# Loads by head and a prologue by head pair in a fused block-sparse attention and gated FFN kernel

## The chip, the cores and the metric

The kernel runs on one core of a Trainium2 chip. The metric is the device time of one execution in microseconds; of several executions the median is taken. TensorE is called PE in the profile (PEld is its weight load), VectorE DVE, ScalarE ACT, GpSimd POOL and SyncE SP.

## What is computed

Attention over 4 batches, 8 heads, 768 positions and head size 64, and behind it a gated feed-forward layer over the 3072 tokens. Each query sees the keys less than 16 positions away, and 24 block summaries of the whole sequence (the maximum of k and the mean of v over blocks of 32 positions):

```python
    k_sum = k.reshape(B, H, nb, block, D).max(axis=3)
    v_sum = v.reshape(B, H, nb, block, D).mean(axis=3)
    scores_l = scale * np.matmul(q, k.transpose(0, 1, 3, 2))
    mask_l = np.abs(pos[:, None] - pos[None, :]) < window
    scores_s = scale * np.einsum('bhsd,bhnd->bhsn', q, k_sum) + np.log(block)
...
    attn = np.matmul(a, np.concatenate([v, v_sum], axis=2))
    # x: attn as [3072, 512]
    ffn_out = gelu(x @ w_gate) * (x @ w_val) @ w_out
    out = x + sigmoid(x @ w_res) * ffn_out
```

Inputs and output are float32 in DRAM; the kernel loads everything as bfloat16[...] and accumulates in float32.

## The kernel before

The work is cut into eight units, half a batch each (384 tokens, six query tiles of 64). For a query tile the keys are its own 64, 16 on each side (the rims) and the 24 summaries, laid side by side in `kW` (128 columns per tile and head pair) and in `vext` (one row per key, for each tile and head 64 values, a column of ones at index 64, and padding up to 96). `kW`, `qT` and `vext` exist twice, for even and odd batches. Heads are handled in pairs: `s_step` computes the transposed scores of one pair for six tiles and their exponentials `P` on ACT, `av_step` (in the first unit `av_first`, in two parts: the band rows, and the summary rows from `vblk`) multiplies by v, `av_end` divides by the sum, and `xt_step` turns the result for the feed-forward part.

The feed-forward part of a unit is twelve steps `fo`. Each step makes a tile g (x times 128 columns of w_gate) and a tile vv (the same of w_val) with four matmuls of 384 columns each; ACT takes the Gelu of g into `ge`, and DVE multiplies by vv into `gvT` (the product of this step). g, vv and several others share four PSUM tiles (`ps_mm`), and `ge` has three buffers. Then come the w_res and w_out matmuls, mixed with the attention of the next unit (`first_out`, `mid_out`). The order on each engine is the order of the program text (`tc.manual_schedule`); each engine works its own queue in order and waits by semaphores.

Unit 0 is special. It has a prologue of its own that turns k and q by PE transposes, makes the block maxima (`k_blocks`) and rims (`k_rims`, `own_rims`) on DVE and the block means by matmul (`vsum_mm`), with `keep_warm` matmuls on a zero tile in between. The band mask `mneg` (0 inside the band, -240000 outside) is built by POOL with four `affine_select`, and is added to the scores of pairs 0 and 1 by a matmul; for pairs 2 and 3 DVE multiplies `P` by `maskt`, which is derived from `mneg`. During the twelve steps of unit 0, `unit0_extras(fo)` puts constants and copies for later onto DVE, behind the product of step `fo`. In the first steps of unit 1, `k_place` puts the turned k of batch 1 in its place. Batches 2 and 3 get k by DMA transposes from `k_nat`.

All loads are issued by POOL in the order of the text: k of batch 0 in two halves by heads, q for the first half sequence, v in twelve blocks of 64 positions (all heads each), the first piece of w_gate among the v blocks; then the pieces of w_val and w_gate in turns, the second q, w_res, w_out, and the data of batch 1.

Of the kernel before, what the change touches and what calls it, by code (L numbers as in the profile page):

```python
# [8 lines left out]
F32 = mybir.dt.float32  # L9
BF16 = mybir.dt.bfloat16  # L10
# [5 lines left out]
def kernel(  # L16
# [50 lines left out]
    mneg = const.tile([128, 128], BF16, name="mneg")  # L67
    vblk = const.tile([128, H, D + 1], BF16, name="vblk")
# [22 lines left out]
    def k_tile():  # L91
        return qk.tile([PP, H, PJ, D], BF16, tag="k_sb", name="k_sb")

    def load_q(half, j):
        t = qk.tile([TU // j, H, j, D], BF16, tag="q_sb", name="q_sb")
        nc.gpsimd.dma_start(
            out=t.rearrange("p h j d -> p h (j d)"),
            in_=q[0, :, half * TU:(half + 1) * TU].rearrange("h (p j) d -> p h (j d)", j=j))
        return t

    def v_loads(b, lo=0, hi=NT):
        for t in range(lo, hi):
            nc.gpsimd.dma_start(out=vext[b % 2][0:QT, t, :, 0:D],  # L103
                                in_=v[b, :, t * QT:(t + 1) * QT, :].rearrange("h p d -> p h d"))
# [9 lines left out]
    def load_k_nat(b):  # L114
        k_nat = qk.tile([QT, NT, DM], BF16, tag="k_nat", name="k_nat")
        for t in range(NT):
            nc.gpsimd.dma_start(out=k_nat[:, t].rearrange("p (h d) -> p h d", d=D),  # L117
                                in_=k[b, :, t * QT:(t + 1) * QT, :].rearrange("h p d -> p h d"))
        return k_nat
# [15 lines left out]
    with tc.manual_schedule():  # L135
# [23 lines left out]
        def load_w(w, src, c):  # L159
# [9 lines left out]
        k_sb[0] = k_tile()  # L169
        load_k(0, k_sb[0], 0, 2)  # L170
        nc.gpsimd.affine_select(out=ident[:], in_=ident[:], compare_op=ALU.not_equal, fill=1.0,
                                base=0, pattern=[[-1, 128]], channel_multiplier=1)
        load_k(0, k_sb[0], 1, 2)
        q_sb[0] = load_q(0, QJ)
        nc.scalar.activation(vext[0][0:QT, :, :, D + 1:VP],
                             warm[0:QT, 0:1].unsqueeze(1).unsqueeze(1).to_broadcast([QT, NT, H, VP - D - 1]),
                             AF.Copy)
        vext_consts(0)
        v_loads(0, 0, 6)
        for cols, sign, base in ((slice(0, QT), 1, WIN - 1), (slice(0, QT), -1, WIN - 1),  # L180
                                 (slice(QT, QT + WIN), 1, WIN - 1 - QT), (slice(QT + WIN, BAND), -1, -1)):
            m = mneg[0:QT, cols]
            nc.gpsimd.affine_select(out=m, in_=m, compare_op=ALU.is_ge, fill=-240000.0, base=base,
                                    pattern=[[-sign, cols.stop - cols.start]], channel_multiplier=sign)
        v_loads(0, 6, 7)
        load_w(w_gate, wg_src, 0)
        v_loads(0, 7, NT)
        kw_consts(0)
        own_keys(bmat, NT)
        nc.vector.memset(vblk[96:128, :, D:D + 1], 1.0)  # L190
        nc.vector.memset(vext[1][0:QT, :, :, D + 1:VP], 0.0)


        for c in range(6):
            if c:
                load_w(w_gate, wg_src, c)
            load_w(w_val, wv_src, c)
            if c == 4:
                q_sb[1] = load_q(1, QJ)
# [53 lines left out]
        def own_rims(lo, hi, after):  # L253
            x = vext[0]
            if after:
                hi = min(hi, NT - 1)
                nc.vector.tensor_copy(x[QT:QT + WIN, lo:hi, :, 0:D], x[0:WIN, lo + 1:hi + 1, :, 0:D])
            else:
                lo = max(lo, 1)
                nc.vector.tensor_copy(x[QT:BAND, lo:hi, :, 0:D], x[QT - 2 * WIN:QT, lo - 1:hi - 1, :, 0:D])  # L260

        def vsum_mm(b, vs, lo, hi):
            for t in range(lo, hi):
                for i in range(2):
                    nc.tensor.matmul(vs[i][96:128, 0:DM // 2], bmat[:, t, :],
                                     vext[b % 2][0:QT, t, 4 * i:4 * i + 4, 0:D],
                                     start=(t == 0), stop=(t == NT - 1))
# [19 lines left out]
        def s_mm(u, hp, s):  # L287
            b, half = u // 2, u % 2
            kw, qt = kW[b % 2], qT[b % 2]
            if u == 0 and hp < 2:  # L290
                for hh in range(2):
                    nc.tensor.matmul(s[hh], mneg[:],
                                     ident[:, 0:QT].unsqueeze(1).to_broadcast([128, HT, QT]),
                                     start=True, stop=False, skip_group_check=True)
            for t in range(HT):
                tt = half * HT + t
                for hh in range(2):
                    ps = slice(hh * 64, hh * 64 + 64)
                    nc.tensor.matmul(s[hh][:, t * QT:(t + 1) * QT], kw[ps, tt, hp, :],  # L299
                                     qt[ps, tt // 2, hp, (tt % 2) * QT:(tt % 2 + 1) * QT],  # L300
                                     start=(u > 0 or hp > 1), stop=True,
                                     skip_group_check=True)

        def s_step(u, hp, st, banks=None):
            if banks:
                s = [p.tile([128, 512], F32, tag=tag, name="s") for p, tag in banks]
            else:
                s2 = ps_s.tile([128, 2, 512], F32, tag="s", name="s")
                s = [s2[:, hh] for hh in range(2)]
            s_mm(u, hp, [x[:, 0:TU] for x in s])  # L310
            P = ppool.tile([128, 2, HT, QT], BF16, tag="P", name="P")
            if banks:
                for hh in range(2):
                    nc.scalar.activation(P[:, hh].rearrange("p t q -> p (t q)"), s[hh][:, 0:TU], AF.Exp,  # L314
                                         scale=scale, bias=bias_t[:])
            else:
                nc.scalar.activation(P.rearrange("p a t q -> p a (t q)"), s2[:, :, 0:TU], AF.Exp,  # L317
                                     scale=scale, bias=bias_t[:])
            if u or hp > 1:
                Pf = P.rearrange("p a t q -> p (a t) q")  # L320
                nc.vector.tensor_mul(Pf, Pf, maskt.unsqueeze(1).to_broadcast([128, 2 * HT, QT]))  # L321
            st["P", hp] = P
# [133 lines left out]

        keep_warm(12)
        k_step(0, 0, ps_mm, "mm")
        k_step(0, 1, ps_mm, "mm")
        keep_warm(6)  # L460
        k_step(0, 2, ps_mm, "mm")
# [3 lines left out]
        k_step(0, 3, ps_mm, "mm")  # L465
        keep_warm(5)
        tq = [turn_pair(q_sb[0], hp, turn_tile(q_sb[0], ps_mm, "mm")) for hp in range(NP)]
        for hp in range(3):
            q_place(0, hp, tq[hp])
        st = new_unit()  # L470
        vs = [ps_t.tile([128, 512], F32, tag="t", name="vs"), ps_o.tile([128, 512], F32, tag="ao", name="vs")]
        s_step(0, 0, st)
        q_place(0, 3, tq[3])
        s_step(0, 1, st, MM2)
        own_rims(0, HT, False)
        own_rims(0, HT, True)
        vsum_mm(0, vs, 0, 3)
        s_step(0, 2, st)
        s_step(0, 3, st, MM2)
        vsum_mm(0, vs, 3, 8)  # L480
        keep_warm(1)
        gvT = upool.tile([128, FO, TU], BF16, tag="gvT", name="gvT")
        ao = [ps_mm.tile([128, NSUB, 2, D + 1], F32, tag="mm", name="ao") for _ in range(NP)]
        for hp in range(3):
            av_first(hp, st, ao[hp], 0, BAND)
        vsum_mm(0, vs, 8, NT)
        nc.vector.tensor_copy(vblk[96:128, 0:H // 2, 0:D],
                              vs[0][96:128, 0:DM // 2].rearrange("p (h d) -> p h d", d=D))
        nc.scalar.copy(vblk[96:128, H // 2:H, 0:D],
                       vs[1][96:128, 0:DM // 2].rearrange("p (h d) -> p h d", d=D))  # L490
        nc.scalar.activation(gate1[:], bias_t[0:1, :], AF.Gelu)
        av_first(3, st, ao[3], 0, BAND)
        keep_warm(1)
        for hp in range(4):
            av_first(hp, st, ao[hp], BAND, 128)
            av_end(hp, st, ao[hp])
        keep_warm(1)
        turn = [dict(pool=ps_t, tag="t", copy=nc.scalar.copy), dict(pool=ps_o, tag="ao", copy=nc.scalar.copy)]
        xt_step(0, 0, st, **turn[0])
        keep_warm(1)  # L500
        xt_step(0, 1, st, **turn[1])
        g0, v0 = mm_tile("g"), mm_tile("vv")
        gv_mm(g0, w_gate, st, 0, (0,))
        gv_mm(v0, w_val, st, 0, (0,))
        xt_step(0, 2, st, **turn[0])
        gv_mm(g0, w_gate, st, 0, (1,))
        gv_mm(v0, w_val, st, 0, (1,))
        g1, v1 = mm_tile("g"), mm_tile("vv")
        gv_mm(g1, w_gate, st, 1, (0, 1))
        xt_step(0, 3, st, **turn[1])  # L510
# [12 lines left out]
        def unit0_extras(fo):  # L523
            if fo == 2:
# [85 lines left out]
        for u in range(NU):  # L610
# [9 lines left out]
            for fo in range(0 if u else 2, FO):  # L620
# [22 lines left out]
                if half == 1 and nb < B:  # L643
# [11 lines left out]
                    if nb == 1:  # L655
                        if fo == 0:
                            tk = turn_all(k_sb[nb])
                        if fo < NP:
                            k_place(nb, fo, tk[fo])
                    elif 2 <= fo < 2 + NP:  # L660
                        k_blocks(nb, fo - 2)
# [36 lines left out]
```

The softmax here doesn't subtract the row's maximum and nothing guards it: scores larger than these inputs give would overflow.

## Time and profile before

| what | value |
|---|---|
| median of 10 runs | 257.25 us (256.88 to 257.84) |
| profiled execution, its own time | 257.4 us |
| its span | 255.6 us |
| PE busy | 248.2 us, 97% of the span |
| DVE busy | 158.0 us, 62% |
| ACT busy | 126.9 us, 50% |
| POOL busy | 111.1 us, 43% |
| v loads (L103) | 48 issues, 741 ns each on POOL |
| k_nat loads (L117) | 24 issues, 732 ns each |
| granted TensorE clock | 9 tenths or more in every slice |

The profile shows one execution. A row of the timeline gives the start and the length in us, the engine, the line of the kernel, the operation, what it writes and reads with their shapes, and in brackets the idle time of the engine before it and what ended it. The chain of waits is the sequence of work that ended last, followed back from the end; a row of it gives the start, the length and who was at work. Busy time of an engine that nobody waits for costs nothing.

### The profile page before, as it was taken

To read this page: it belongs to the slowest core of one execution; us is meant where nothing else is said; L and a number is where in the kernel's file an instruction comes from. 1 tells how busy PE (TensorE), PEld (TensorE's weight loads), DVE (VectorE), ACT (ScalarE), POOL (GpSimd) and SP (SyncE) were. 2 spreads that over 40 slices of the span, in tenths; PEclk is the share of its full clock that TensorE was granted. 3 is DMA by queue.
4 is the path that set the end of the run, shared out by engine and by line. 5 is a ranking of instruction groups with operands and counts; after the bars stand their busy time and mean duration, and the time that the engine had idled before them with its cause. 6 is when DMAs were issued, how large, how long until landed. Compare 5 with 4: busy or idle time off the path is not lost.

```text
span 255.6 us, 5803 instructions
## 1 busy us (share of the span) xinstructions
PE 248.2 (97%) x2277; PEld 138.4 (54%) x2300; DVE 158.0 (62%) x350; ACT 126.9 (50%) x212; POOL 111.1 (43%) x155
## 2 busy tenths in 40 slices
PE   8999999999999999999999999999999999999994
PEld 2665654565554555546654665545554565455543
DVE  5975776399477544767567544867567544854424
ACT  6676359266493338344482338244482337253320
POOL 8897552293345986265405995157404000000000
PEclk9999999999999999999999999999999999999999
DMA  5999999999913999989603999959903500240003
GB/s 79 179 141 169 197 201 208 191 163 184 144 22 98 170 109 146 121 136 178 120 13 95 177 112 153 103 132 165 139 15 78 136 0 3 50 138 0 0 3 123
DMA packets 98475, 29.34 MB, mean 115 GB/s; under 512 B 83592, under 2 KB 95312, under 8 KB 98352
## 3 DMA queue, kind: packets, MB, share of 16 engines
q0 software_dynamic: 68720, 14.76, 69.2%
q1 hardware_dynamic: 29728, 14.21, 24.9%
q8 instruction: 18, 0.29, 0.5%
q14 instruction: 9, 0.07, 0.1%
HBM read 29.36 MB, written 6.29 MB: 139 GB/s over the span
## 4 chain that ended last, share of the span: by engine, by line
PE 80%; DMA 10%; DVE 4%; POOL 3%; issue 2%; POOLq 0%; DVEq 0%
PE f L423 23%; PE vv L375 21%; PE g L375 21%; PE r L413 8%; DMA w_val<-in_moe_w_val_dram 4%; DMA w_gate<-in_moe_w_gate_dram 3%; PE ao L335 3%; DMA q_sb<-in_q_dram 3%; PE s L299 3%; POOL vext L103 2%; DVE th L429 1%; DVE o L432 1%; PE vs L273 1%; POOL w_val L161 1%; POOL w_gate L161 1%
## 5 line engine op out<-in xcount | busy, mean ns | idle before, releaser
L381 DVE TENSOR_TENSOR gvT<-ge,vv 128x384 bf16<-128x384 f32 x96 | 52.6, 552 | 50.7 <-PE vv L375 46.3
L380 ACT ACTIVATE ge<-g 128x384 f32<-128x384 f32 x96 | 46.9, 490 | 69.4 <-DVE gvT L381 36.4
L375 PE MATMUL vv<-xT,w_val 128*128 128x384 bf16 x384 | 78.7, 326 | 0.4 <-DMA w_val<-in_moe_w_val_dram 0.3
L375 PE MATMUL g<-xT,w_gate 128*128 128x384 bf16 x384 | 78.8, 326 | 0.1
L423 PE MATMUL f<-w_out,gvT 128*128 128x512 bf16 x262 | 62.7, 380 | 1.5 <-issue 1.1
L375 PEld LDWEIGHTS <-w_gate 128*128 128x128 bf16 x384 | 37.1, 98 | 26.7 <-issue 1.8
L375 PEld LDWEIGHTS <-w_val 128*128 128x128 bf16 x384 | 37.4, 98 | 25.4 <-DMA w_val<-in_moe_w_val_dram 0.7
L423 PEld LDWEIGHTS <-gvT 128*128 128x128 bf16 x276 | 25.6, 98 | 29.6 <-DMA w_out<-in_moe_w_out_dram 0.3
L103 POOL DMA_DIRECT2D vext<-in_v_dram x48 | 33.5, 741 | 13.4 <-DMA w_out<-in_moe_w_out_dram 5.6
L416 ACT ACTIVATE th<-r 128x512 f32<-128x512 f32 x24 | 13.5, 605 | 27.5 <-PE r L413 27.5
L429 DVE SCALAR_TENSOR_TENSOR th<-th,f 128x512 f32<-128x512 f32 (+2 forms) x26 | 16.6, 640 | 14.1 <-PE f L423 14.1
L321 DVE TENSOR_TENSOR P<-P,maskt 128x768 bf16<-128x768 bf16 x30 | 17.1, 572 | 11.2 <-ACT P L317 6.1
L413 PE MATMUL r<-w_res,xT 128*128 128x512 bf16 x88 | 22.7, 380 | 0.4
L285 POOL COPY vext<-vsum 32x1536 bf16<-32x1536 bf16 x12 | 17.2, 1463 | 12.9 <-DMA vsum<-vpart 12.8
L432 DVE SCALAR_TENSOR_TENSOR o<-th,xn 128x512 f32<-128x512 f32 (+2 forms) x26 | 18.4, 709 | 0.9
L355 DVE TENSOR_TENSOR xn<-ao,rz 128x384 bf16<-128x384 f32 x32 | 17.8, 557 | 1.1
L317 ACT ACTIVATE P<-s,bias_t 128x768 bf16<-128x768 f32 x17 | 15.3, 902 | 4.3 <-PE s L299 4.1
L117 POOL DMA_DIRECT2D k_nat<-in_k_dram x24 | 16.4, 732 | 1.7 <-DMA k_nat<-in_k_dram 0.9
L123 POOL DMA_DIRECT2D q_nat<-in_q_dram x18 | 15.9, 923 | 0.7 <-issue 0.7
L314 ACT ACTIVATE P<-s,bias_t 128x384 bf16<-128x384 f32 x30 | 15.7, 580 | 0.0
L228 DVE TENSOR_REDUCE ks<-kW 128x24 bf16<-128x768 bf16 x16 | 15.1, 943 | 0.4 <-ACT kW L243 0.4
L413 PEld LDWEIGHTS <-xT 128*128 128x128 bf16 x96 | 8.8, 98 | 9.9
(83 smaller groups left out, 173.0 us busy)
## 6 DMA issues: line engine op xcount, KB each, us to landing
out_dram<-o SPq DMA_DIRECT2D x23, 256.0 KB, 2.2
vext<-in_v_dram POOLq DMA_DIRECT2D x48, 64.0 KB, 6.4
q_nat<-in_q_dram POOLq DMA_DIRECT2D x18, 128.0 KB, 6.9
w_gate<-in_moe_w_gate_dram POOLq DMA_DIRECT2D x6, 256.0 KB, 7.9
w_val<-in_moe_w_val_dram POOLq DMA_DIRECT2D x6, 256.0 KB, 8.8
w_out<-in_moe_w_out_dram POOLq DMA_DIRECT2D x3, 512.0 KB, 14.3
k_nat<-in_k_dram POOLq DMA_DIRECT2D x24, 64.0 KB, 4.6
vext<-vext SPq DMA_DIRECT2D x6, 144.0 KB, 5.4
```

The costliest lines, as they stand in the source:

```text
L103: nc.gpsimd.dma_start(out=vext[b % 2][0:QT, t, :, 0:D], in_=v[b, :, t * QT:(t + 1) * QT, :].rearrange("h p d -> p h d"))
L117: nc.gpsimd.dma_start(out=k_nat[:, t].rearrange("p (h d) -> p h d", d=D), in_=k[b, :, t * QT:(t + 1) * QT, :].rearrange("h p d -> p h d"))
L285: eng.tensor_copy(vext[b % 2][96:128, lo:hi, :, 0:D], src)
L321: nc.vector.tensor_mul(Pf, Pf, maskt.unsqueeze(1).to_broadcast([128, 2 * HT, QT]))
L355: nc.vector.tensor_mul(xn, ao[:, :, :, 0:D], rz.to_broadcast([128, NSUB, 2, D]))
L375: nc.tensor.matmul(ps[:, 0:TU], w[:, ko, fo * 128:(fo + 1) * 128], st["xT"][:, ko, :], start=(ko == 0), stop=(ko == KO - 1), skip_group_ch ...
L380: nc.scalar.activation(ge[:], g[:, 0:TU], AF.Gelu)
L381: nc.vector.tensor_mul(gvT[:, fo, :], ge[:], vv[:, 0:TU])
L413: nc.tensor.matmul(r[:], st["xT"][:, ko, ss], w_res[:, ko, :], start=(ko == 0), stop=(ko == KO - 1))
L423: nc.tensor.matmul(st["f", sub][:], gvT[:, fo, ss], w_out[:, fo, :], start=(fo == 0), stop=(fo == FO - 1), skip_group_check=True)
L429: nc.vector.scalar_tensor_tensor(th[:, cs], th[:, cs], 1.0, f[:, 0:n], ALU.add, ALU.mult)
L432: nc.vector.scalar_tensor_tensor(o.rearrange("p (k d) -> p k d", d=128), th[:, cs].rearrange("p (k d) -> p k d", d=128), 0.5, x, ALU.mult, ...
```

## The change

k and q of batch 0 come by halves of heads in turns (k heads 0 to 3, q heads 0 to 3, k heads 4 to 7, q heads 4 to 7). v, in every batch, and `k_nat`, in batches 2 and 3, come by head, eight loads instead of twelve. All eight v loads of batch 0 stand ahead of the first piece of w_gate.

The band mask is made on DVE: an identity shifted by one column is widened by five maxima of shifted copies in a new tile `band`, and three `tensor_scalar` write `mneg` from it. The four `affine_select` on `mneg` go. In unit 0 all four pairs get the mask by matmul, and DVE masks no `P` there.

The prologue is rewritten as four chains, one per head pair: turning k and q, scores, rims (`pair_rims`), block means (`vsum_pair`), the band part and the summary part of av, `av_end` and `xt_step` follow one another per pair, interleaved by hand; six of the `keep_warm` matmuls go. The constant padding of `vext[1]` (`memset` of columns 65 to 95) moves from the start of the kernel into `unit0_extras` of steps 2 to 5, three tiles at each. In unit 1, `k_place` runs at steps 0, 2, 4 and 6 in the pair order 2, 0, 1, 3, instead of at steps 0 to 3.

```diff
+    band = const.tile([128, 2, 128], BF16, name="band")
...
+    def v_loads(b):
+        for h in range(H):
+            nc.gpsimd.dma_start(out=vext[b % 2][0:QT, :, h, 0:D],
+                                in_=v[b, h].rearrange("(t p) d -> p t d", p=QT))
...
-        for t in range(NT):
-            nc.gpsimd.dma_start(out=k_nat[:, t].rearrange("p (h d) -> p h d", d=D),
-                                in_=k[b, :, t * QT:(t + 1) * QT, :].rearrange("h p d -> p h d"))
+        for h in range(H):
+            nc.gpsimd.dma_start(out=k_nat[:, :, h * D:(h + 1) * D],
+                                in_=k[b, h].rearrange("(t p) d -> p t d", p=QT))
...
         load_k(0, k_sb[0], 0, 2)
...
+        load_q(0, q_sb[0], 0, 2)
         load_k(0, k_sb[0], 1, 2)
-        q_sb[0] = load_q(0, QJ)
+        load_q(0, q_sb[0], 1, 2)
+        v_loads(0)
+        load_w(w_gate, wg_src, 0)
...
+        nc.vector.memset(band[0:QT], 0.0)
         vext_consts(0)
-        v_loads(0, 0, 6)
-        for cols, sign, base in ((slice(0, QT), 1, WIN - 1), ...):
-            m = mneg[0:QT, cols]
-            nc.gpsimd.affine_select(out=m, in_=m, compare_op=ALU.is_ge, fill=-240000.0, base=base,
-                                    pattern=[[-sign, cols.stop - cols.start]], channel_multiplier=sign)
-        v_loads(0, 6, 7)
-        load_w(w_gate, wg_src, 0)
-        v_loads(0, 7, NT)
+        own_keys(bmat, NT)
+        nc.vector.tensor_copy(band[0:QT, 0, 33:128], ident[0:QT, 0:95])
+        for i, d in enumerate((1, 2, 4, 8, 15)):
+            nc.vector.tensor_tensor(out=band[0:QT, (i + 1) % 2, 32:128], in0=band[0:QT, i % 2, 32:128],
+                                    in1=band[0:QT, i % 2, 32 - d:128 - d], op=ALU.max)
+        for cols, lo in ((slice(0, QT), WIN), (slice(QT, QT + WIN), WIN + QT), (slice(QT + WIN, BAND), 0)):
+            nc.vector.tensor_scalar(out=mneg[0:QT, cols],
+                                    in0=band[0:QT, 1, 32 + lo:32 + lo + cols.stop - cols.start],
+                                    scalar1=-1.0, scalar2=240000.0, op0=ALU.add, op1=ALU.mult)
         kw_consts(0)
-        own_keys(bmat, NT)
         nc.vector.memset(vblk[96:128, :, D:D + 1], 1.0)
-        nc.vector.memset(vext[1][0:QT, :, :, D + 1:VP], 0.0)
...
+        def pair_rims(hp):
+            own_rims(0, HT, False, slice(2 * hp, 2 * hp + 2))
+            own_rims(0, HT, True, slice(2 * hp, 2 * hp + 2))
+
+        def vsum_pair(hp, pool, tag, copy):
+            vs = pool.tile([128, 512], F32, tag=tag, name="vs")
+            hs = slice(2 * hp, 2 * hp + 2)
+            for t in range(NT):
+                nc.tensor.matmul(vs[96:128, 0:2 * D], bmat[:, t, :], vext[0][0:QT, t, hs, 0:D],
+                                 start=(t == 0), stop=(t == NT - 1))
+            copy(vblk[96:128, hs, 0:D], vs[96:128, 0:2 * D].rearrange("p (h d) -> p h d", d=D))
...
-            if u == 0 and hp < 2:
+            if u == 0:
...
-            if u or hp > 1:
+            if u:
                 Pf = P.rearrange("p a t q -> p (a t) q")
                 nc.vector.tensor_mul(Pf, Pf, maskt.unsqueeze(1).to_broadcast([128, 2 * HT, QT]))
...
         keep_warm(12)
+        k_step(0, 0, *mm)
+        k_step(0, 1, *mm)
+        q_step(0, *mm)
+        q_step(1, *mm)
...
         keep_warm(5)
+        k_step(0, 2, *mm)
+        k_step(0, 3, *mm)
         s_step(0, 0, st)
         s_step(0, 1, st, MM2)
+        t2 = [q_turn(2, *mm), q_turn(3, *mm)]
+        vsum_pair(0, ps_t, "t", nc.scalar.copy)
+        q_place(0, 2, t2[0])
+        q_place(0, 3, t2[1])
         keep_warm(1)
+        pair_rims(0)
+        vsum_pair(1, ps_o, "ao", nc.scalar.copy)
...
+        pair_rims(1)
+        av_band(0)
+        av_blk(0)
+        s_step(0, 2, st)
+        av_band(1)
+        s_step(0, 3, st, MM2)
+        pair_rims(2)
+        av_blk(1)
+        vsum_pair(2, ps_t, "t", nc.scalar.copy)
+        nc.scalar.activation(gate1[:], bias_t[0:1, :], AF.Gelu)
         keep_warm(1)
+        av_band(2)
+        pair_rims(3)
+        vsum_pair(3, ps_o, "ao", nc.vector.tensor_copy)
+        av_blk(2)
         xt_step(0, 0, st, **turn[0])
+        av_band(3)
         keep_warm(1)
+        av_blk(3)
         xt_step(0, 1, st, **turn[1])
+        keep_warm(1)
...
...
         def unit0_extras(fo):
+            if fo < 6:
+                ts = slice(3 * fo - 6, 3 * fo - 3)
+                nc.vector.memset(vext[1][0:QT, ts, :, D + 1:VP], 0.0)
             if fo == 2:
                 vext_consts(1)
...
-                        if fo < NP:
-                            k_place(nb, fo, tk[fo])
+                        if fo in (0, 2, 4, 6):
+                            hp = (2, 0, 1, 3)[fo // 2]
+                            k_place(nb, hp, tk[hp])
```

## The prediction

> **What bounds the kernel now.** I read the page first, then the chain of waits, then the timeline of VectorE and of GpSimd in the first 40 us, because every edit but the smaller number of load instructions lies there. PE is busy for 97% of the span, so from the first gate matmul on a change is worth only what it adds to or takes from PE's stalls. The chain says what holds PE before that:
>
> ```profile
> PE 248.2 (97%) x2277; PEld 138.4 (54%) x2300; DVE 158.0 (62%) x350; ACT 126.9 (50%) x212; POOL 111.1 (43%) x155
> ```
>
> ```profile
> 11.37 3.89 POOL vext L103 x5
> 15.26 1.06 POOL w_val L161
> ...
> 17.78 7.34 DMA w_gate<-in_moe_w_gate_dram
> 25.12 0.28 issue
> 25.40 11.36 DMA w_val<-in_moe_w_val_dram
> 36.76 0.04 issue
> 36.80 0.82 PE vv L375 x4
> ```
>
> The reader is to see that the last w_val piece lands at 36.76 (25.40 + 11.36) and PE uses it at 36.80. The g matmuls before it start at 35.71 and need 4 x 0.1625 = 0.65, so PE was free at 36.36: it loses 0.44 us there. Until then PE and the stream of loads run neck and neck. The other half is VectorE:
>
> ```profile
> 5.24 2.54 DVE L191 MEMSET vext<- 64x2976 bf16 x1 [0.66 <-issue]
> 8.17 0.95 DVE L228 TENSOR_REDUCE ks<-kW 128x24 bf16<-128x768 bf16 x1 [0.39 <-ACT kW L243]
> ```
>
> ```profile
> 25.98 0.56 DVE L381 TENSOR_TENSOR gvT<-ge,vv 128x384 bf16<-128x384 f32 x1 [0.46 <-PE vv L375]
> 26.89 0.14 DVE L138 MEMSET vext<- 128x96 bf16 x1 [0.35 <-issue]
> 27.19 0.49 DVE L139 MEMSET vext<- 32x520 bf16 x1 [0.17 <-DVE vext L138]
> ...
> 27.88 0.49 DVE L141 MEMSET vext<- 16x520 bf16 x1
> 28.40 0.55 DVE L381 TENSOR_TENSOR gvT<-ge,vv 128x384 bf16<-128x384 f32 x1
> ...
> 29.60 0.50 DVE L381 TENSOR_TENSOR gvT<-ge,vv 128x384 bf16<-128x384 f32 x1
> 30.13 0.43 DVE L285 COPY vext<-vblk 32x1024 bf16<-32x1024 bf16 x1
> 30.59 0.56 DVE L381 TENSOR_TENSOR gvT<-ge,vv 128x384 bf16<-128x384 f32 x1
> ```
>
> The big memset of vext[1] lies where VectorE has nothing else: it ends at 7.78, and VectorE then idles 0.39 us for ACT. From 26 us on VectorE has no idle time that it could give: the products gvT follow the other small work directly.
>
> **The change part by part.**
>
> *Loads.* Before, k (two halves), q, seven v blocks, w_gate 0 and five v blocks; GpSimd keeps at most eight loads in flight, for each issue waits for the landing of the eighth before it (w_gate at 10.60 for q, landed 10.31). In the trace the k halves land at 6.44 and 8.35 (1.91 each), q 1.97 later, v blocks 0.44 apart, the last at 17.60; weight pieces take 1.31 when nothing disturbs. After: k 6.44, q half 7.42, k 9.33, q 10.31, then eight v heads of 96 KB at 0.66 each (pieces of the same 128 bytes, hence the same rate): 11.0 to 15.6. GpSimd issues 768 pieces in 0.78 us (the q_sb row), so eight v loads take 6.3 instead of 12 x 0.74 = 8.9, and the four affine selects on mneg (0.93) leave it. Between 16.5 and 17.5 the stream ran dry, since the last v load and w_val 0 took 1.20 and 1.07 to issue; that hole should go. The weights then land some 1.0 to 1.7 us earlier: 15.6 + 12 x 1.31 + 1.97 = 33.3 for the last w_val, plus the 1.5 to 2.5 that the before's stream lost to other dips, is 34.8 to 35.8 against 36.76. That pays only the 0.44 us, because PE isn't ready earlier, as follows.
>
> *Prologue order.* I worked the before's program forward in its own order, from its own durations: an instruction starts when its engine is free and its inputs are there, 0.235 us from the last matmul to its reader, 0.05 between other engines, 0.095 for PE to change tile shape (all read from the trace). It puts the first matmul of the last quarter of fo 0 at 23.49; the trace has 23.51. The same rule for the new order: ACT copies k0, k1 (0.70 each), q0, q1 (0.375 each) until 9.37; k2 waits for its load (9.38); P0 11.38, P1 until 13.13, the vsum copies and q2, q3 until 14.38; VectorE finishes the four k_blocks at 13.85 (1.42 each) and does rims of pairs 0 and 1 (0.64 each, scaled from 0.82 and 1.00 for all heads) until 15.13; PE starts av of pair 0 at 14.57; P3 ends at 17.94; the Gelu table load (1.28 + 0.20) follows vsum 2 and ends at 19.77; first gate matmul 21.06 (before: 21.03); last quarter 23.57. So the prologue gains nothing: what is saved on waiting for all of v (vsum ended at 18.2) is paid back by four vsum passes, 48 matmuls of 128 columns for 24 of 256, two more band-mask pairs (0.33 each) and more changes of shape. Value: -0.06. With rims and vsum 30% dearer it is -0.75; with both 20 to 30% cheaper, +0.3; the v loads may come 0.9 later before they count.
>
> *Band mask.* One memset, one copy, five maxima of 64x96 and three tensor_scalar. No row has a 64x96 maximum; the nearest are 0.17 for the 128x64 tensor_scalar (L464) and 0.20 for the 128x176 copy. Ten such with 0.03 between are 2.3 at most, 1.0 at least. VectorE is through at about 6.0, the transpose of mneg is due at 7.9: nothing, covered by the wait for k's first copy; without the cover at most 0.4. The masking of P2 and P3 by VectorE (2 x 0.56) goes; that is counted in the order above.
>
> *The memset of vext[1].* Its 2976 columns move to fo 2 to 5 of unit 0, 744 at each, behind the product of that fo. Price: the row's duration gives 2.54/4 = 0.63; with the idle time in front, (2.54 + 0.66)/4 = 0.80. The Trainium skill, VectorE: DVE Perf Modes, section "Zero memsets can be issued as uint32 (trn2)", says that a memset takes one cycle per element whatever the type and that only whole 4-byte words can be packed; runs of 31 bf16 can't be. At the 0.96 GHz of its Specifications that is 0.78, an estimate, which sides with the idle time being part of the work. I take 0.80; were the idle time a fixed price of each memset, it would be 1.3. Then VectorE, from the end of product 2 at 26.54: product 3 ends at 29.75 (before 28.95), 4 at 31.7, 5 at 33.6, 6 at 35.4 (before 32.20). Four PSUM tiles serve g and vv, and three ge tiles the Gelu, so vv of fo n+3 can't run before product n has ended: vv of fo 7 was at 31.56, of fo 8 at 32.86, of fo 9 at 34.16, and waits until 35.4. PE is held up by 1.3 us in all (0.6 at a price of 0.63, 3.3 at 1.3). Queued behind it are all matmuls of the kernel. In the windows view VectorE is busy 9.53 of the 12 us from 25 to 37; 3.2 more is 12.7.
>
> *GpSimd's lock.* The skill, SBUF — State Buffer, section "Who interferes with whom", says that a VectorE copy in a two-port mode shuts GpSimd out for the whole instruction. The trace bears it out in size: issues of 1.20 and 1.07 instead of 0.70 beside the rim copies of 0.82 and 1.00 at 14.16 and 15.01. The rims are now eight copies of about 0.32 in the stretch where the weights are issued: by the rule up to 2.6 us, by the row (0.9 for 1.8 of copying) 1.3. Either is hidden, because from the 18th load on an issue waits for a landing anyway.
>
> *Later.* k_nat and v of later batches by head: 4 issues fewer per tensor, some 2.6 us of GpSimd each, no gain, since after 62 us no PE wait in the waits view is on a load; a slower rate from the new stride would be hidden by a unit's 28 us. k_place at fo 0, 2, 4, 6 instead of 0 to 3: PE lost 0.26 at 58.75 behind the first k_blocks and the product of fo 1, which stay in that order: nothing, at best 0.26.
>
> **Sum.** +1.3 (memsets) + 0.06 (prologue) - 0.44 (the w_val wait, hidden then) = +0.9 on the span of 255.6. The profiled execution took 257.4, 1.8 more than its span and 0.15 above the median of 257.25; so 258.1.
>
> **Rivals.**
> *The earlier stream wins (faster).* Place: the wait at 36.80 and the chain through vsum. If pairs start as their heads land and rims and vsum cost less than I scaled, the prologue gains 0.3; if a memset costs 0.63, PE loses 0.6 and has 0.44 back: 0.1 faster; with no hold-up of PE at all (a build that hands out PSUM tiles so that a late product costs nothing), 0.7 faster, 256.5. It decides where the hold-up falls below 0.44 plus the prologue's gain. For it: the hole at 16.5 to 17.5. Against it: VectorE's row from 26 to 33 has no idle time. Chance 0.17; 256.5.
> *They cancel.* Price 0.63 with the prologue as worked: +0.2, 257.4. Chance 0.25.
> *The pairs are late too.* v by head at a lower rate (another stride in DRAM; no row shows one): heads 2 us later put the last quarter at 24.75, 1.2 more; with the memsets, 259.3. Chance 0.13.
> *Likeliest:* the memsets' backlog, 257.8 to 258.8. Chance 0.45.
>
> **Numbers.** 0.2% is 0.51 us, about what this kernel's times can tell. Faster than 256.74: 0.17; within: 0.25; slower than 257.76: 0.45 + 0.13 = 0.58. The range leaves out the better half of the fast case and the worst of the late one: 256.6 to 259.5.
>
> **What would show it.** Right: four memsets of 64x744 on VectorE of about 0.63 with idle time before them, product 6 of unit 0 ending some 9 us after product 2 (before 5.7), PE idle at vv of fo 8 and 9, no PE wait on w_val; v's last head landing near 15.6; first gate matmul at 21.1. Wrong: PE unbroken from fo 2 to fo 9, or a first gate matmul before 20.5 or after 22.

## The result and the profile after

The changed kernel takes 264.53 us (median of 9 runs, 262.58 to 265.73) where the kernel before takes 257.21 beside it (32 runs): a ratio of 1.028, with a 95% interval of 1.0265 to 1.030. It is 7.3 us slower; 258.1 was predicted, and the range ended at 259.5. A ratio here leaves out single executions that stand over 1.5% above the others of their kernel; in this case those are executions in which TensorE's clock fell, and they are named where they matter.

The profiled execution took 263.94 us with a span of 262.1, so these lines stand against 255.6. First, of the page of after, the row of busy times and the clock row of the 40 slices (6.55 us each; a digit is tenths of full speed):

```profile
PE 251.8 (96%) x2299; PEld 141.7 (54%) x2322; DVE 162.0 (62%) x368; ACT 127.0 (48%) x213; POOL 97.1 (37%) x128
...
PEclk9985899999999999999999999999999999999999
```

The 5 in the fourth slice is new: before it is 9 throughout. The windows view of after (length of the stretch, busy time of each engine, granted clock, DMA share, GB/s) puts a number on it:

```profile
core 0: us, PE busy (x) PEld busy (x) DVE busy (x) ACT busy (x) POOL busy (x), PEclk, DMA share, GB/s
6.00:21.00 15.00, 12.66 (x257) 8.59 (x259) 12.12 (x45) 9.84 (x18) 12.08 (x17) 0.89 1.77 182
21.00:25.00 4.00, 4.00 (x56) 2.96 (x56) 1.25 (x4) 1.23 (x3) 2.29 (x3) 0.50 1.45 194
25.00:37.00 12.00, 11.91 (x68) 6.81 (x67) 6.46 (x28) 4.28 (x9) 5.99 (x8) 0.87 1.39 200
```

The same view of before has, for the second of these stretches:

```profile
21.00:25.00 4.00, 3.91 (x29) 2.26 (x27) 1.60 (x5) 2.31 (x5) 2.80 (x4) 1.00 1.38 181
```

PE looks fully busy from 21 to 25, and yet it does half the work: it runs at 0.50. In the clock's own record the low stretch reaches from 17.81 to 28.05, 10.24 us. In before the clock is 1.00 in all these stretches. The busy share does not show this here; the column of the clock does. In the chain of waits of after, the twelve block-sum matmuls of pair 2 take 1.39 inside the stretch; in e10 below, at full clock, they take 0.77 to the start of the next instruction (17.68 to 18.45):

```profile
18.57 1.39 PE vs L284 x12
```

PE's timeline of after shows what came before the clock fell:

```profile
13.64 0.83 PE L284 MATMUL vs<-vext,bmat 64*32 64x128 bf16 x12 [0.31 <-DMA vext<-in_v_dram]
15.61 0.38 PE L366 MATMUL ao<-vext,P 96*64 96x65 bf16 x12 [1.14 <-DVE vext L271]
```

PE finished the block sums of pair 1 (their last result is modelled to 14.47) and was idle for 1.14 us, until VectorE had copied the rims of pair 0 (15.55). VectorE's and GpSimd's timelines of after show why the rims were late:

```profile
14.11 0.69 DVE L274 COPY vext<-vext 32x640 bf16<-32x640 bf16 x1
14.84 0.71 DVE L271 COPY vext<-vext 16x768 bf16<-16x768 bf16 x1
15.58 0.71 DVE L274 COPY vext<-vext 32x640 bf16<-32x640 bf16 x1
16.32 0.35 DVE L271 COPY vext<-vext 16x768 bf16<-16x768 bf16 x1
```

```profile
13.87 0.76 POOL L165 DMA_DIRECT2D w_val<-in_moe_w_val_dram  x1
14.60 0.77 POOL L165 DMA_DIRECT2D w_gate<-in_moe_w_gate_dram  x1
15.33 0.78 POOL L165 DMA_DIRECT2D w_val<-in_moe_w_val_dram  x1
17.28 0.74 POOL L165 DMA_DIRECT2D w_gate<-in_moe_w_gate_dram  x1 [1.17 <-DMA vext<-in_v_dram]
```

In these rows a copy takes 0.35 when GpSimd stands still (the one at 16.32) and 0.69 to 0.71 when GpSimd is issuing a load. Each of the three slow ones ends a little under 0.2 after an issue ends: 14.80, 15.55 and 16.29 against 14.63, 15.37 and 16.11.

Last, VectorE's timeline of after in the first steps of unit 0 that follow. The four memsets are there as predicted:

```profile
31.45 0.55 DVE L400 TENSOR_TENSOR gvT<-ge,vv 128x384 bf16<-128x384 f32 x1 [0.57 <-PE vv L394]
32.10 0.68 DVE L556 MEMSET vext<- 64x744 bf16 x1
...
34.64 0.55 DVE L400 TENSOR_TENSOR gvT<-ge,vv 128x384 bf16<-128x384 f32 x1
35.29 0.68 DVE L556 MEMSET vext<- 64x744 bf16 x1
...
37.22 0.68 DVE L556 MEMSET vext<- 64x744 bf16 x1
...
38.38 0.55 DVE L400 TENSOR_TENSOR gvT<-ge,vv 128x384 bf16<-128x384 f32 x1
39.02 0.68 DVE L556 MEMSET vext<- 64x744 bf16 x1
...
40.18 0.56 DVE L400 TENSOR_TENSOR gvT<-ge,vv 128x384 bf16<-128x384 f32 x1
```

Where the time came in, by the start of the same matmul in both traces, first in before, then in after:

```profile
21.03 0.32 PE L375 MATMUL g<-xT,w_gate 128*128 128x384 bf16 x1
```

```profile
25.39 0.53 PE L394 MATMUL g<-xT,w_gate 128*128 128x384 bf16 x1
```

The first gate matmul is at 25.39 (before 21.03), that of fo 2 at 29.88 (24.42), of fo 10 at 42.33 (35.71), of unit 1 at 58.81 (52.36), of unit 7 at 232.57 (226.05). So 4.4 us are lost before the first gate matmul, 1.1 more until fo 2, 1.2 more until fo 10, and nothing that counts afterwards.

My theory after this comparison had three terms: a clock drop set off by a hole on PE (some 4 us), that hole itself, which comes from rim copies held up by GpSimd's issues (put at 1.3), and the memsets (put at 1.2 to 1.4). Rivals: the four-chain order of the prologue is itself slow, or the clock fell by chance and would have fallen in the kernel before too.

### The profile page after: what moved, and what is told of

Its sections match the earlier page's. It is cut to its first block, busy times and chain, and to the rows that moved or that the text cites. A ratio compares the mean times of both kernels' runs of the same rounds, so it can differ in the third digit from the quotient of the medians.

```text
span 262.1 us, 5837 instructions
## 1 busy us (share of the span) xinstructions
PE 251.8 (96%) x2299; PEld 141.7 (54%) x2322; DVE 162.0 (62%) x368; ACT 127.0 (48%) x213; POOL 97.1 (37%) x128
## 4 chain that ended last, share of the span: by engine, by line
PE 86%; DVE 6%; issue 2%; DMA 2%; ACT 1%; POOL 1%; POOLq 0%; DVEq 0%; ACTq 0%
PE g L394 22%; PE vv L394 22%; PE f L442 22%; PE r L432 8%; PE ao L354 3%; PE s L318 3%; DMA k_sb<-in_k_dram 2%; PE ao L366 1%; PE vs L284 1%; DVE gvT L400 1%; PE vs L292 1%; PE xp L379 1%; DVE vext L274 1%; DVE vext L556 1%; PE tp L219 1%
## 5 line engine op out<-in xcount | busy, mean ns | idle before, releaser
L394 PE MATMUL g<-xT,w_gate 128*128 128x384 bf16 x384 | 79.6, 328 | 0.1
L107 POOL DMA_DIRECT2D vext<-in_v_dram x32 | 24.4, 788 | 15.2 <-DMA w_out<-in_moe_w_out_dram 5.1
L340 DVE TENSOR_TENSOR P<-P,maskt 128x768 bf16<-128x768 bf16 x28 | 16.4, 587 | 9.8 <-ACT P L336 4.9
L372 DVE RECIPROCAL rz<-ao 128x6 f32<-128x6 f32 x32 | 6.1, 191 | 11.3 <-PE ao L354 9.9
```

Of the source, the lines that this page charges most:

```text
L107: nc.gpsimd.dma_start(out=vext[b % 2][0:QT, :, h, 0:D], in_=v[b, h].rearrange("(t p) d -> p t d", p=QT))
L394: nc.tensor.matmul(ps[:, 0:TU], w[:, ko, fo * 128:(fo + 1) * 128], st["xT"][:, ko, :], start=(ko == 0), stop=(ko == KO - 1), skip_group_ch ...
```

## The experiments

**e1_fill: fill the hole.** Of after, with

```diff
         vsum_pair(1, ps_o, "ao", nc.scalar.copy)
+        keep_warm(6)
```

> The kernel after, with keep_warm(6) put behind vsum_pair(1), that is six matmuls (1.3 us) into the hole of 1.3 us in which PE waits for the rims of pair 0. Clock theory (the hole let the granted clock fall to 0.5 for 10 us, which costs some 4.5 us): no half-clock stretch, first gate matmul near 21 to 21.5, 259.5 to 260.3 us. Long-prologue theory (the order itself is slow, the clock only follows): no change, 264.5, or up to 1.3 slower. Backlog theory alone (the memsets): no change, 264.5.

260.07 us (259.87 to 260.86, 4 runs), ratio 1.012 [1.011, 1.014]. The windows view of e1_fill:

```profile
6.00:21.00 15.00, 13.12 (x268) 8.49 (x270) 11.75 (x45) 9.71 (x18) 12.01 (x17) 1.00 1.76 180
21.00:25.00 4.00, 3.97 (x67) 2.67 (x65) 1.89 (x6) 2.31 (x5) 2.29 (x3) 1.00 1.45 197
```

Six matmuls on zeros, which compute nothing, make the kernel 4.5 us faster: the clock stays at 1.00. The drop is an effect of the hole, and it is the largest term. Two things in this profile make e12 below the cleaner test. Here the rims of pair 0 are done at 15.70, only 0.4 after the block sums (which end at 15.27), so without the fill the hole would have been shorter than in after, and the fill holds av up until 16.60. The reason is in VectorE's and GpSimd's timelines of e1:

```profile
14.81 0.35 DVE L274 COPY vext<-vext 32x640 bf16<-32x640 bf16 x1
15.19 0.51 DVE L271 COPY vext<-vext 16x768 bf16<-16x768 bf16 x1
```

```profile
14.77 0.76 POOL L165 DMA_DIRECT2D w_val<-in_moe_w_val_dram  x1
```

The first copy starts 0.04 after an issue and is not stretched; the second starts 0.42 into the same issue and ends 0.17 after it.

**e2_memset_act and e3_before_memset: the memsets alone.** In e2, after without the four memsets, ScalarE zeroing the padding of `vext[1]` at the start; in e3, before with only the memset moved:

```diff
-        nc.vector.memset(vext[1][0:QT, :, :, D + 1:VP], 0.0)
...
+            if fo < 6:
+                ts = slice(3 * fo - 6, 3 * fo - 3)
+                nc.vector.memset(vext[1][0:QT, ts, :, D + 1:VP], 0.0)
```

> The kernel after, with the padding of vext[1] written by ScalarE in one piece at the start (it idles there until 7.1 us) instead of four memsets of VectorE in steps 2 to 5 of unit 0. Backlog theory: the PE holes at the vv of steps 5 to 9 (0.31, 0.51, 0.28 and 0.17 in the trace of after, 1.1 to 1.3 us in all) go, 263.2 to 263.5; if a wait for w_val takes their place, 263.8. Clock theory: the stretch at half clock stays, the gain is the same 1.1. If the memsets are hidden: 264.5.

> The kernel before, with only the memset of vext[1] moved into steps 2 to 5 of unit 0, as the change does. Backlog theory: +1.3 less the 0.44 wait for w_val that it hides, 258.0 to 258.3; VectorE's gvT of step 6 ends near 35.4 instead of 32.2. If the memsets are hidden: 257.2.

e2: 263.09 (261.29 to 263.81, 4 runs), 1.4 less than after, with the clock still at half speed (15.59 to 29.24 in its profile). The two kernels also differ by 1.4 to 1.5 among executions of like mean clock: 262.58 to 263.94 in after against 261.29 and 262.56 at 0.978 to 0.980, 264.46 to 265.73 against 263.61 and 263.81 at 0.972 to 0.974. e3: 258.28 (258.07 to 258.54), ratio 1.005 [1.004, 1.006], 1.2 more than before (257.09 beside it). PE's timeline of e3 shows where it waits:

```profile
33.73 0.81 PE L374 MATMUL vv<-xT,w_val 128*128 128x384 bf16 x4 [0.39 <-DVE gvT L380]
34.37 0.81 PE L374 MATMUL g<-xT,w_gate 128*128 128x384 bf16 x4
35.52 0.81 PE L374 MATMUL vv<-xT,w_val 128*128 128x384 bf16 x4 [0.34 <-DVE gvT L380]
```

vv waits for the product three steps back. No matmul of e3 waits for w_val: as predicted, the wait of before hides behind this one. The g matmuls of fo 10 start 1.36 later than in before (37.07, before 35.71), those of fo 11 0.92 later (38.38, before 37.46). With or without the new prologue the moved memset costs 1.2 to 1.4, in e3 after the hidden wait is taken off.

**e4_pool_waits: GpSimd still while the rims are copied.** Of after, with the loads behind w_val 0 (the other weights and the second q) moved behind a one-element GpSimd copy that waits for the rims of pair 1:

```diff
-        for c in range(6):
-            if c:
-                load_w(w_gate, wg_src, c)
...
+        load_w(w_val, wv_src, 0)
...
         pair_rims(1)
+        nc.gpsimd.tensor_copy(gate2[:], vext[0][QT:QT + 1, 1, 2, 0:1])
+        for c in range(6):
+            if c:
+                load_w(w_gate, wg_src, c)
...
         av_band(0)
```

> The kernel after, with GpSimd held before the second piece of w_gate until the rims of pair 1 are copied, so that it issues nothing while VectorE copies the rims of pairs 0 and 1. Lock theory (GpSimd's descriptor writing makes these copies take 0.70 instead of 0.35): the four copies take 0.35, av of pair 0 starts at 14.9 instead of 15.6, the hole on PE shrinks from 1.3 to 0.6 us; with the clock theory the clock then stays up more often, 260 to 264. Without the lock: copies still 0.7, time 264.5, or later by what the held loads cost.

Four executions: 258.52, 259.12, 259.92 and 264.35; without the last a ratio of 1.0085 [1.0055, 1.0115]. VectorE's and PE's timelines of e4:

```profile
14.57 0.35 DVE L263 COPY vext<-vext 32x640 bf16<-32x640 bf16 x1
14.96 0.35 DVE L260 COPY vext<-vext 16x768 bf16<-16x768 bf16 x1
15.34 0.35 DVE L263 COPY vext<-vext 32x640 bf16<-32x640 bf16 x1
15.72 0.35 DVE L260 COPY vext<-vext 16x768 bf16<-16x768 bf16 x1
16.11 0.20 DVE L361 RECIPROCAL rz<-ao 128x6 f32<-128x6 f32 x1
16.34 0.56 DVE L363 TENSOR_TENSOR xn<-ao,rz 128x384 bf16<-128x384 f32 x1
16.93 0.65 DVE L263 COPY vext<-vext 32x640 bf16<-32x640 bf16 x1
```

```profile
14.47 0.83 PE L273 MATMUL vs<-vext,bmat 64*32 64x128 bf16 x12 [0.40 <-DMA vext<-in_v_dram]
15.36 0.38 PE L355 MATMUL ao<-vext,P 96*64 96x65 bf16 x12
```

All four copies now take 0.35, and av follows the block sums at once, though the copies start later than in after (14.57 for 14.11). The one at 16.93, when GpSimd issues again, takes 0.65. So it is the issues that stretch the copies. The hole is gone, and with it the drop in three of four executions; the fourth had a mean clock of 0.971.

**e6_before_nowarm6: is a hole dangerous in the kernel before too?** Of before, without the `keep_warm(6)` between the second and third `k_step`.

> The kernel before without the keep_warm(6) that the change also takes out, so that PE has a hole of 1.3 us near 7.6 to 8.9 us and nothing else changes. Rival to the hole at 14 us: it was the missing six matmuls that let the clock fall. In that case a stretch at half clock appears here as well, 260 to 262. If the hole behind the rims was the cause: no such stretch, 257.1, unchanged.

257.56 (20 runs), ratio 1.002 [1.0007, 1.003]. I expected no low stretch, and that was wrong. PE's timeline and the windows of e6:

```profile
6.44 0.87 PE L211 MATMUL tp<-ident,k_sb 96*64 96x96 bf16 x32
8.36 0.53 PE L211 MATMUL tp<-ident,k_sb 96*64 96x96 bf16 x16 [1.05 <-DMA k_sb<-in_k_dram]
```

```profile
6.00:9.00 3.00, 1.73 (x51) 1.17 (x49) 2.90 (x4) 1.57 (x3) 2.85 (x8) 1.00 1.32 200
9.00:13.00 4.00, 4.00 (x52) 2.15 (x54) 3.93 (x13) 1.98 (x4) 3.09 (x5) 0.57 2.16 163
```

A hole in which PE is idle for 1.05 us is followed by a low stretch from 9.38 to 12.79, 3.41 us. By their mean clock (0.987 to 0.993, the others 0.997 or more) 13 of the 20 executions had such a stretch. The first gate matmul comes 0.8 later (21.80), and 0.44 of that is taken back by the wait for w_val that before has anyway (fo 11 at 37.79, before 37.46). This settles two things: such a hole drops the clock in another place of another program, and the six fills of before stand in the way of that. In PE's timeline of before they fill the place:

```profile
7.57 1.25 PE L455 MATMUL wp<-warm 128*128 128x512 bf16 x5
```

**e7_before_heads_later and e8_before_dve_mask: other parts done alone in before.** e7: `k_nat` and v of batches 1 to 3 by head. e8: band mask by VectorE, padding by ScalarE, all of v ahead of w_gate 0.

```diff
-                v_loads(nb)
+                v_heads(nb)
```

> The kernel before with k_nat of batches 2 and 3 and v of batches 1 to 3 loaded by head (8 loads instead of 12 each), batch 0 as it was. Theory: hidden, 257.1 within 0.3. Rival (the stride of 16 KB between a head's tiles slows the stream, or the rims of v wait for whole heads): 257.6 or more.

```diff
-        v_loads(0, 0, 6)
...
-            nc.gpsimd.affine_select(out=m, in_=m, compare_op=ALU.is_ge, fill=-240000.0, base=base,
...
-        v_loads(0, 6, 7)
+        v_loads(0)
         load_w(w_gate, wg_src, 0)
-        v_loads(0, 7, NT)
+        nc.vector.tensor_copy(band[0:QT, 0, 33:128], ident[0:QT, 0:95])
...
```

> The kernel before with the mask part alone: band mask by VectorE instead of four affine selects, all of v (twelve blocks) ahead of the first piece of w_gate, and the padding of vext[1] by ScalarE at the start in place of VectorE's memset. Theory: the last v load lands about 1 us earlier than 17.60, vsum follows it, the first gate matmul moves from 21.03 to 20.2 to 20.6, the weights come earlier by as much: 256.2 to 256.8. If PE or ACT bounds the old prologue anyway: 257.1. If ScalarE's 2.7 us delay its k copies: 257.4.

e7: 257.17, ratio 1.0002 [0.9994, 1.001]: hidden, as predicted. e8: 258.22, ratio 1.005 [1.003, 1.0065], slower where I expected 256.2 to 256.8. The prologue did end earlier (first gate matmul 20.53), but the weights came later, as PE's timeline of e8 shows at fo 10:

```profile
35.89 0.82 PE L380 MATMUL g<-xT,w_gate 128*128 128x384 bf16 x4 [0.23 <-DMA w_gate<-in_moe_w_gate_dram]
37.28 0.82 PE L380 MATMUL vv<-xT,w_val 128*128 128x384 bf16 x4 [0.57 <-DMA w_val<-in_moe_w_val_dram]
```

w_val 5 landed at 37.23 (before 36.76). Between 17 and 23 us three weight pieces took 1.9 to 2.4 where others take 1.3.

**e9_all_three, e10_pool_memset and e12_fill3: the three cures together.** e9 is after with the edits of e1, e2 and e4; e10 is e9 without `keep_warm(6)`; e12 is after with `keep_warm(3)` in place of e1's six.

> The kernel after with three repairs: keep_warm(6) in the hole, the padding of vext[1] by ScalarE at the start, GpSimd held during the rims of pairs 0 and 1. If the clock, the backlog and the lock are all that the change costs: 257.0 to 257.9, no stretch at half clock, no hole on PE behind the products of steps 2 to 5. If a fourth cost is in the new order: 258.5 or more.

> The kernel after with GpSimd's next loads held until the rims of pair 1 are copied, and the padding of vext[1] zeroed by ScalarE at the start; no fill matmuls. Theory: of e9 the six fill matmuls lie on the path once nothing is waited for there, 6 x 0.213 = 1.28; without them the first gate matmul is at about 22.1 as in e4 and fo 2 at about 25.5, with no memsets behind it: 258.72 - 1.25 = 257.5 (257.2 to 258.0), with the granted clock at 1.0 from 6 us on. Rival: the fill was needed to hold the clock, and without it some executions show a stretch at half clock: 259 or more, scattered. What is left against before is then the prologue's order alone, about a microsecond at the first gate matmul less the 0.44 that before waits for w_val.

> The kernel after with three fill matmuls behind the second pair's block sums, half the fill of e1. The hole there shrinks from 1.3 us to about 0.65. If the length of that hole decides on the granted clock, and 0.65 is short enough, the clock stays at 1.0 and the time is that of e1, 259.8 to 260.6. If any hole of that place or the sum of idle time in the prologue decides, a stretch at 0.5 remains: 262 to 264.5, or executions of both kinds.

e9: 258.72 (258.37 to 259.29), ratio 1.007 [1.005, 1.008], 0.8 above the highest that I expected. The reason is in PE's timeline of e9; the rims of pair 0 were done at 15.36:

```profile
15.20 1.47 PE L466 MATMUL wp<-warm 128*128 128x512 bf16 x6
16.59 0.38 PE L358 MATMUL ao<-vext,P 96*64 96x65 bf16 x12
```

With the hole gone, the fill itself lies on the path. e10 shows its price: 257.46 us, 1.26 less than e9, six times 0.21, and against before (257.34 beside it) a ratio of 1.0003 [0.9993, 1.001]. The whole loss is accounted for. But one of its 14 executions took 263.07, at a mean clock of 0.974.

e12: 259.46, 0.6 less than e1, three times 0.2, and no drop, though PE still waits in that place:

```profile
14.67 0.82 PE L474 MATMUL wp<-warm 128*128 128x512 bf16 x3
16.07 0.38 PE L366 MATMUL ao<-vext,P 96*64 96x65 bf16 x12 [0.58 <-DVE vext L271]
```

This is the clean test of the clock: the first three rim copies take 0.69 to 0.71 as in after, the rims of pair 0 are done at 16.01, and the fill ends before them, so that it costs nothing and hardly anything but the clock differs from after. The clock is worth 5.1 us (264.53 less 259.46), more than e1's 4.5, in which the end of the fill lay on the path. e12 and e10 in turn price the held-up copies: in both profiles the clock is full and the block sums of pair 1 start alike (13.91 and 14.00), but av of pair 0 starts at 16.07 and 15.03, and fo 2 at 26.19 and 25.14. That is 1.05. From fo 2 to fo 10 (38.63 and 36.43) the memsets add 1.15.

**e11_before_mask_order and e13_no_single_fills: is there a version that beats both?** e11 is e8 with w_gate 0 back behind the seventh v tile; e13 is e10 without three single `keep_warm(1)` that ran with everything behind them ready.

> The kernel before with the band mask built by VectorE and the padding of vext[1] zeroed by ScalarE, the loads left in the order of before (seven v tiles, w_gate 0, five v tiles). Theory: e8 lost because its first weights landed later (w_gate 0 at 18.78, w_val 0 at 21.21) through the order of the loads; with w_gate 0 ahead of the last five v tiles the weights come as in before or a little earlier, and w_val 5 at 36.3 or earlier: 256.3 to 257.0. Rival: the loads without the four affine_selects between them bunch into the same slow stretch whatever their order, and the first w_val lands after 20.5: 257.5 to 258.3 as in e8.

> The kernel of e10 without three single fill matmuls (behind the third pair's block sums, behind the band part of pair 3 and behind the second turn of the output), which in e10 run with everything behind them ready. Theory: they lie on the path, 0.32 + 0.32 + 0.21 with the idle time at their edges, so the first gate matmul comes at about 20.9 in place of 21.76; of that w_val's last piece, at about 36.5, takes back some 0.3 at fo 10: 256.7 to 257.2, by 0.1 to 0.25% under before. Rival: without them the granted clock falls in more of the executions, whose times then scatter to 262 and more; or something else is waited for behind them, and the time stays at 257.3 to 257.6.

e11: 257.39, ratio 1.0004 [0.9992, 1.0015], where I expected 256.3 to 257.0. The position of w_gate 0 was e8's loss, but the freed VectorE and GpSimd time buys nothing. e13: 257.10 against 256.97, ratio 1.0002 [0.999, 1.0014]. Its first gate matmul is at 21.00 as expected (e10: 21.76), 0.55 of it is left at unit 2, and in the profiled execution units 2 and 4 give that back: they take 0.24 and 0.39 longer than in e10, of which the profile shows 0.25 as idle time of PE, and the rest is open. Two of its 14 executions took 262, and a third, 258.15, had a mean clock of 0.993. Nothing that I ran beats before.

**e14_narrow24 and e15_narrow12: what of the hole counts?** The six wide fills of e1 replaced by as much time of narrow ones, 24 in e14; in e15 12, as long as e12's three:

```diff
+        def keep_narrow(n):
+            wp = ps_s.tile([128, 2, 512], F32, tag="s", name="wp")
+            for _ in range(n):
+                nc.tensor.matmul(wp[96:128, 0, 0:128], warm[0:64, 0:32], warm[0:64, 0:128], start=True, stop=True)
...
         vsum_pair(1, ps_o, "ao", nc.scalar.copy)
+        keep_narrow(24)
```

> The kernel after with 24 narrow matmuls (64 rows by 32 columns of the array, 128 columns of zeros) where e1 has six wide ones (128 by 128, 512 columns): by the row of the block sums (12 in 0.62) some 1.25 us, so PE is as busy as in e1. If the clock follows PE's idle time, it stays at 1.0 and the time is that of e1, 259.5 to 260.5. If it weighs how much of the array works, narrow matmuls do not hold it: a stretch at 0.5 and 262 to 265, in most executions.

> The same with 12 narrow matmuls, 0.62 us, as long as the three wide ones of e12, which held the clock with 0.74 us of the hole left. By idle time: as e12, 259.2 to 259.9 at 1.0. By the share of the array: 262 to 265.

e14: 259.80, 259.81, 259.84 and 265.11; e15: 258.82, 259.22, 260.00 and 264.95. Narrow matmuls mostly hold the clock, so idle time is the larger part of the cause. They may hold it less surely than wide ones: over all kernels with wide fill in that place (e1, e9, e12) none of 12 executions stood apart from the others, of those with narrow fill 2 of 8, of those with no fill but no long hole (e4, e10, e13) 4 of 32, and with the hole (after, e2) all 13 lie above 261. So few executions don't settle whether the share of the array counts as well. Of the two profiles only that of e14 has the long hole under its fill (block sums to 14.69, rims of pair 0 done at 16.04); in that of e15 the first copy starts 0.09 after an issue and isn't stretched, as in e1, and av follows the fill at once.

## Why the prediction was wrong

*The sum had no term for the clock.* This is the failed step, and the largest. I worked the prologue's order out from durations taken at full clock, and took PE's idle time there as worth its length and no more. The first gate matmul was to come at 21.06; it came at 25.39, which the prediction itself had named as a sign that it was wrong (after 22). With the clock held up by a fill that costs nothing itself (e12), 5.1 of the 7.3 us are gone. The 259.46 that remain lie just inside the range, still 1.4 above 258.1, for reasons that follow.

The Trainium skill, TensorE: Matmul & The Clock Gate, says in "What's actually happening" that the clock is decided in free-running windows of 4096 cycles at 1.2 GHz, 3.41 us; in "HAM oscillation — how this bites in real kernels" it gives the rule of no idle gap on PE over some 3.4 us. The first agrees with these traces: the low stretches last 3.41 (e6), 10.24 (after, three times 3.413) and 13.65 (e2, four times). The second would have let holes of 1.05 to 1.16 us of idle time (e6, after, e2) pass; the runs show that they don't, and the measurement decides. I laid windows of 3.413 us from the rise of the clock on each trace, and summed PE's idle time in them. The window that ends at the drop has 1.14 us (after, 14.40 to 17.81), 1.18 (e2) and 1.27 (e6). Windows with 0.91 (e1) and 1.00 (e9) were passed at full clock. It isn't a clean threshold: the very first window after the rise has 1.29 in after, 1.25 in e12 and 1.09 in e7, and no drop follows, while e6's 1.27 lies in such a first window too. Since the windows do not start with the program (the clock rises at 4.0 to 7.2 us from one profile to the next), a hole may be split between two of them; that would explain why the same program drops in some executions and not in others, as in e4, e10 and e13. That was argued from the grid, not tried.

*GpSimd's lock was taken in one direction only.* The prediction said that the rim copies would delay GpSimd's issues, and that either price was hidden. The other direction decided: issues of 0.74 to 0.78 stretched copies of 0.35 to 0.70, and PE waited for the copies. av of pair 0 was put at 14.57 and came at 15.61. The price on the path is 1.05 (e12 against e10), which the sum had at nothing. The section "Who interferes with whom" of SBUF — State Buffer says that whichever of the two starts first shuts the other out for its whole length; I had used half of it. The traces agree in part. In the ten profiles of after and its variants, a rim copy that starts up to 0.20 after the start of an issue takes 0.35, although the issue started first; one that starts 0.23 or more into it does not end before the issue does, and where it is stretched ends 0.14 to 0.19 after it. So whether the rims are late depends on where the copies fall between the issues, and differs from execution to execution (e1 and e15).

*The memsets were right.* Price 0.80 each: measured 0.68 with about 0.1 around it. The estimate of 0.78 from the skill's page is above the measured length, and the measurement decides. The hold-up predicted as 1.3 is 1.36 at fo 10 of e3, 1.15 between e12 and e10 and 1.4 in e2; product 6 ends 8.7 us after product 2 (32.00 to 40.74), predicted some 9. That no matmul would then wait for w_val held too. But of the result it is a fifth.

*The prologue's order is dearer than worked out, by 0.7.* With the clock at full speed and no copies held up (e10) the first gate matmul is at 21.76 instead of 21.06. PE is idle for 0.64 before k's second half, which landed at 9.84 there (9.44 in after) and not at 9.33; and three single fills lie on the path (e13, without them: 21.00). The rival of late pairs had the right symptom, a late start of av, for a wrong reason, the rate of the v loads: the last two heads did land late, as follows, but PE doesn't wait for them.

*Loads.* The last v head was put at 15.6 and landed at 17.48; heads came every 0.7 or so as worked out, one took 1.1, and after the sixth (14.85) nothing landed until 17.00. That is no hole in the stream. The windows view of after for this stretch, and that of before for the dip that the prediction read at 16.5 to 17.5:

```profile
14.85:17.00 2.15, 1.40 (x42) 0.94 (x44) 2.02 (x5) 0.00 (x0) 1.26 (x2) 1.00 1.66 190
```

```profile
16.50:17.50 1.00, 1.00 (x40) 0.86 (x40) 0.66 (x2) 0.32 (x1) 1.00 (x2) 1.00 0.75 50
```

In before the stream did run dry, at 50 GB/s, and in after that is gone, as predicted (196 GB/s from 17.00 to 18.20). What moves from 14.85 to 17.00 in after are mostly the pieces of w_gate and w_val: of 1041 packets only 316 are under 512 B, as those of v are. So the last pieces of v arrive among the weights. e10, in which GpSimd issues nothing from 13.36 to 15.89, has the same (15.03 to 17.29, 190 GB/s); why these few pieces are so late stays open. The last w_val piece landed at 34.88, inside the 34.8 to 35.8 given, and was worth nothing, as no matmul was ready for it.

*Band mask and later loads.* VectorE's mask is through at about 6.0 and hidden; the later loads by head are worth nothing (e7). Both as predicted.

The accounts: 5.1 (clock, after less e12) + 1.05 (held-up copies) + 1.15 (memsets) = 7.3 of 7.3. The last two are read from the profiles of e12 and e10, whose medians differ by 2.0; e10, with all three undone, is at before's time.

## What to carry to other kernels

Give every hole that a reordering opens on TensorE a second price beside its length: what follows runs at half speed if the clock falls, so bound each PE wait of a microsecond or more in a prologue from that side, and do not take out a fill matmul before knowing what it covers. A short VectorE copy on the path should not fall among GpSimd's load issues (0.35 became 0.7 here); hold the issues, or move the copy. And a fill matmul is free only as long as there is a hole under it (three cost nothing in e12, six cost 1.26 in e9): when the hole is cured, take the fill out.

## What was unexpected of the hardware

- Holes in which PE was idle for 1.05 to 1.16 us were enough for the granted clock to go to 0.50, for 3.41, 10.24 or 13.65 us. One window of 3.41 us more at half speed costs about 1.7 (after at a mean clock of 0.972 to 0.974 against 0.980: 264.46 to 265.73, 262.58 to 263.94). Why one hole costs one window (e6) and another three or four, although PE is busy in nearly all of that time, is open.
- bf16 copies on VectorE of 32x640 and 16x768 took 0.35 alone, and up to 0.71 beside GpSimd's load issues of 0.74 to 0.86. A start up to 0.20 after the issue's start escaped; one at 0.23 did not.
- Loads can land late in a stream that does not pause: no v head landed for 2.15 us in after, and for 2.26 in e10, while 190 GB/s flowed.
